# Attention on one core: a slot plan for the other matmuls, five rotating score banks, six value visits per group

## The chip, the core and the metric

The kernel runs on one core of one Trainium2 chip. The metric is the device time of one execution in microseconds (us), taken as the median of several runs. TensorE (PE) multiplies, ScalarE (ACT) evaluates exponentials and casts, VectorE (DVE) and GpSimd (POOL) do elementwise work, and SyncE (SP) issues nearly all transfers. PE writes its results to PSUM, of which a core has eight banks of 128 x 512 float32 values.

## The reference

```python
def _A_ref(x, wq, wk, wv, wo):                     # x: 1 x 2048 x 448, 16 heads of 28
    q = (x @ wq).reshape(B, S, H, Dh).transpose(0, 2, 1, 3)
    k = x @ wk                                     # one key and one value head for all
    v = x @ wv
    scores = jnp.einsum("bhqd,bkd->bhqk", q, k) * (Dh ** -0.5)
    p = softmax(scores, axis=-1)
    o = jnp.einsum("bhqk,bkd->bhqd", p, v)
    return o.transpose(0, 2, 1, 3).reshape(B, S, H * Dh) @ wo

def _B_ref(x, w1, w2, w3, w4):
    h = gelu(layernorm(x) @ w1)
    hs = shift_four_channel_quarters(h, +1, -1, +2, -2) @ w2
    x1 = x + hs
    return x1 + gelu(layernorm(x1) @ w3) @ w4      # 448 -> 1792 -> 448

g = sigmoid((x * gate_w).sum(-1, keepdims=True))
return g * _A_ref(...) + (1 - g) * _B_ref(...)
```

## The kernel before

The first 424 us of the profiled execution compute keys, values, the query projections of the first two groups and all of branch B; `x1` then holds branch B. The change leaves these stages alone. What follows is attention, in the part of the kernel that opens the pools `s3` and `ps3`.

**Groups and key tiles.** Attention is cut into NU = 16 groups `u`: four blocks `b` of 512 queries times four head groups `g` of four heads. In a group the loop runs over NT = 16 key tiles `kt` of 128 keys. For each key tile and each of the four heads `j`, PE computes one score tile `s` (128 keys x 512 queries, line 663), and ACT writes its exponential `p` to SBUF (line 665). Scores and weights are in float32r, products with values in float32.

**Value products.** `pv_group` (lines 618 to 636) multiplies the four `p` tiles of one key tile with `vext` (values and a column of ones) into the four 32-row strips of one PSUM bank `pv` (line 625). The four heads use four column strips of the array. The loop calls it for two key tiles at a time, in every second turn, for the key tiles that lie two and three turns back (LAG = 2, PVB = 2). Such a call is called a visit below: eight visits per group, 16 instruction records each (each product has two records).

**PSUM.** Two banks `mm`, one `misc`, one `mx` (for `pv`), two `m` and two `s`. Score tile n goes to one of five banks by n modulo 5 (`s_tile`; both `mm`, `misc`, both `s`). In the last group it is three banks (n modulo 3), since two `m` and two `s` banks hold the four output accumulators of the last block.

**PE's other work in attention.** PE's order is the order of the program text (`manual_schedule`); the other engines are ordered by the scheduler. Between scores PE has: the 11 matmuls of a query projection (`q_job`, line 503) for the group after the next, whose result is split by ACT and DVE (`q_evac`) and copied by three transfers into `qs`; four parts of the row maximum of the next group (`max_part`, four small matmuls each, line 166, reduced by DVE on line 167), then `max_end` on DVE and one transposing matmul in `max_rows` (line 193); one matmul that spreads the reciprocal sums (`norm_job`, line 543); and for each block four tiles of 12 matmuls of the output projection (`wo_job`, lines 556 to 560), each closed by `gate_out`. All of these use the two `m` banks. `pump()` takes one step of the queue `jobs` after every second score tile. Query jobs are put at the head of the queue; the four output tiles of a block come in one run after the block's last group; the max parts stand outside the queue at key tiles 6 to 9.

**Start of attention.** `wqraw`, block 0 of x (`xq_0`) and `woraw` are loaded to two buffers of tag `raw` and split by DVE and POOL (`split_wq`, `load_x`, lines 485 to 490 and 577 to 593). The later blocks of x are loaded by `load_x` half a group ahead.

**End.** After the last group the bank `pv` is copied by ACT in four parts, transposed, scaled, transposed again and multiplied with the last group's part of `wo` (`tail_a`, `tail_b`, `tail_c`); nine of the twelve matmuls of each output tile of the last block have been done before, in the last group.

Of the kernel before, what the change touches and what calls it, by code (L numbers as in the profile page):

```python
# [15 lines left out]
P = 128  # L16
# [13 lines left out]
LAG = 2  # L30
PVB = 2
# [4 lines left out]
def f32(ap):  # L36
    return ap.bitcast(F32)
# [3 lines left out]
def gated_mix_kernel(  # L41
# [412 lines left out]
    with tc.tile_pool(name="s3", bufs=1, reuse_waits="tile") as s3, \  # L454
# [14 lines left out]
        def s_more(name):  # L469
            return ps3.tile([P, 512], F32, tag="s", bufs=2, name=name)  # L470

# [11 lines left out]
        def load_x(b):  # L483
            raw = s3.tile([P, 4, 512], F32, tag="raw", bufs=2, name=f"xq_{b}")
            nc.sync.dma_start(raw, xT[:, :, 512 * b:512 * b + 512])
            ah = s3.tile([P, 4, 512], F32R, tag="ah", bufs=1, name=f"ahq_{b}")
            al = s3.tile([P, 3, 512], F32R, tag="al", bufs=1, name=f"alq_{b}")
            (nc.gpsimd if b else nc.vector).tensor_copy(ah, raw)
            nc.gpsimd.tensor_tensor(al, raw[:, 0:3, :], f32(ah)[:, 0:3, :], ALU.subtract)
            nc.gpsimd.tensor_tensor(ah[64:128, 3, :], raw[64:128, 3, :], f32(ah)[64:128, 3, :], ALU.subtract)  # L490
            xact[b] = (ah, al)

        def q_job(u):
            b, g = divmod(u, NG)
            ah, al = xact[b]
            cols = slice(g * P, (g + 1) * P)
            ps = misc_tile(f"q_{u}")
            ops = []
            for c in range(3):
                ops += [(wqh[:, c, cols], ah[:, c, :]), (wqh[:, c, cols], al[:, c, :]), (wql[:, c, cols], ah[:, c, :])]  # L500
            ops += [(wqh[:, 3, cols], ah[:, 3, :]), (wql[:, 3, cols], ah[:, 3, :])]
            for n, (w, a) in enumerate(ops):
                nc.tensor.matmul(ps, w, a, start=(n == 0), stop=(n == 10))  # L503
                if n < 10:
                    yield
# [3 lines left out]
            yield  # L509
# [31 lines left out]
        def norm_job(u, o, rb):  # L541
            ps = (mm_tile if u == NU - 2 else misc_tile)(f"rbc_{u}")
            nc.tensor.matmul(ps, sel8, rb, start=True, stop=True)
            on = s3.tile([P, 512], F32, tag="onf", bufs=2, name=f"on_{u}")
            nc.vector.tensor_mul(on, o, ps)  # L545
            onh = s3.tile([P, 512], F32R, tag="onh", bufs=5, name=f"onh_{u}")
            onl = s3.tile([P, 512], F32R, tag="onl", bufs=5, name=f"onl_{u}")
# [3 lines left out]
            yield  # L551

        def wo_group(ps, b, t, g, first, last):
            tok = slice(t * P, (t + 1) * P)
            onh, onl = on_of[b * NG + g]
            nc.tensor.matmul(ps, onh[:, tok], woh[:, g, :], start=first, stop=False)  # L556
            yield
            nc.tensor.matmul(ps, onh[:, tok], wol[:, g, :], start=False, stop=False)  # L558
            yield
            nc.tensor.matmul(ps, onl[:, tok], woh[:, g, :], start=False, stop=last)  # L560

# [5 lines left out]
        def wo_job(b, t):  # L567
            ps = misc_tile(f"wo_{b}_{t}")[:, 0:D]
            for g in range(NG):
                yield from wo_group(ps, b, t, g, g == 0, g == NG - 1)  # L570
                if g < NG - 1:
                    yield
            gate_out(4 * b + t, ps)
            yield

        wqraw = s3.tile([P, 4, 512], F32, tag="raw", bufs=2, name="wqraw")
# [10 lines left out]
        split_wq(2, 4)  # L587
        load_x(0)
        woraw = s3.tile([P, 4, 512], F32, tag="raw", bufs=2, name="woraw")[:, :, 0:D]
        nc.sync.dma_start(woraw, wo.rearrange("(g p) n -> p g n", p=P))  # L590
        split_wq(0, 2)
# [6 lines left out]
        jobs = []  # L598
        current = [None]

        def pump():
            if current[0] is None:
                if jobs:
                    current[0] = jobs.pop(0)()
                    next(current[0])
            else:
                try:
                    next(current[0])
                except StopIteration:
                    current[0] = None  # L610

        def drain():
            while current[0] is not None or jobs:
                pump()
# [3 lines left out]
        def pv_group(k):  # L618
            u, kt = divmod(k, NT)
            if kt == 0:  # L620
                pv_of[u] = max_tile(f"pv_{u}")
            pv = pv_of[u]
            ps = p_of.pop(k)
            for j in range(4):
                nc.tensor.matmul(pv[32 * j:32 * j + 32, :], vext[:, kt, :], ps[j],  # L625
                                 start=(kt == 0), stop=(kt == NT - 1), tile_position=(0, 32 * j))
            if kt == NT - 1 and u < NU - 1:
                o, rb = recip_begin(u, pv_of.pop(u))
                delayed.append((k + 6, lambda: norm_job(u, o, rb)))
                if u == NU - 2:  # L630
                    for t in range(4):
                        delayed.append((k + 10, lambda t=t: wo_last_job(t, NG - 2)))
                elif u % NG == NG - 1:
                    for t in range(4):
                        delayed.append((k + 8, lambda t=t: wo_job(u // NG, t)))

        wo_last = []

        def wo_last_job(t, g):
            if g == 0:  # L640
                wo_last.append((m_tile if t < 2 else s_more)(f"wo_{NB - 1}_{t}")[:, 0:D])
            yield from wo_group(wo_last[t], NB - 1, t, g, g == 0, False)
            yield

        delayed = []
        for k in range(NU * NT + LAG):
            u, kt = divmod(k, NT)
            while delayed and delayed[0][0] <= k:
                jobs.append(delayed.pop(0)[1])
            if k == (NU - 1) * NT:  # L650
                for g in range(NG - 2):
                    for t in range(4):
                        jobs.append(lambda t=t, g=g: wo_last_job(t, g))
            if k < NU * NT:
                if kt == (7 if u == 0 else 2) and u + 2 < NU:
                    jobs.insert(0, lambda u=u: q_job(u + 2))
                if kt == 8 and (u + 3) % NG == 0 and u + 3 < NU:
                    load_x((u + 3) // NG)
                p_of[k] = []
                for j in range(4):  # L660
                    n = 4 * k + j
                    ps = s_tile(n, u == NU - 1)
                    nc.tensor.matmul(ps, kS[0:98, kt * P:(kt + 1) * P], q_of[u][0:98, j, :], start=True, stop=True)  # L663
                    p = s3.tile([P, 512], F32, tag="p", bufs=4 * (LAG + PVB) + 2, name=f"p_{n}")
                    nc.scalar.activation(p, ps, AF.Exp, scale=SCALE)  # L665
                    p_of[k].append(p)
                    if j % 2 == 1 or u == NU - 1:
                        pump()
                if u + 1 < NU:
                    if 6 <= kt < 10:  # L670
                        max_part(u + 1, kt - 6, m_tile)
                    elif kt == 10:
                        max_end(u + 1)
                    elif kt == 11:
                        max_rows(u + 1, m_tile)
# [4 lines left out]
        assert not delayed  # L680
        drain()
# [4 lines left out]
        onh = s3.tile([P, 512], F32R, tag="onh", bufs=5, name=f"onh_{u}")  # L686
        onl = s3.tile([P, 512], F32R, tag="onl", bufs=5, name=f"onl_{u}")
# [20 lines left out]
        def tail_c(t):  # L708
            for _ in wo_group(wo_last[t], NB - 1, t, NG - 1, False, True):
                pass  # L710
            gate_out(4 * (NB - 1) + t, wo_last[t])
# [22 lines left out]
        with tc.If(again > 0):  # L734
            for b in range(NB):
                load_x(b)
                for g in range(NG):
# [7 lines left out]
                    for kt in range(NT):  # L745
                        for j in range(4):
# [3 lines left out]
                            p = s3.tile([P, 512], F32, tag="p", bufs=4 * (LAG + PVB) + 2, name=f"p2_{u}_{kt}_{j}")  # L750
# [59 lines left out]
```

## Time and profile before

| | |
|---|---|
| runs | 1069.8, 1070.5, 1071.85 us; median 1070.5 us |
| profiled execution | 1070.98 us, of which its span (first to last instruction) 1069.1 us |
| mean granted TensorE clock | 0.987 of full speed |
| busy: PE, ACT, DVE, POOL | 1039.7, 673.2, 258.0, 159.8 us |
| attention | the first score starts at 423.94 us |

A line of the timeline reads: start, duration of the merged run of equal instructions, engine, line of the kernel, operation, output <- inputs, shapes, number; in brackets the idle time before it and what ended it. PE's durations overlap, since matmuls are pipelined: the distance of two starts is what an instruction costs PE. In a line of the stages, each engine has its busy time and instruction count, then come the granted clock, the share of busy DMA engines and GB/s.

### The profile page before, as it was taken

To read this page: it belongs to the slowest core of one execution; us is meant where nothing else is said; L and a number is where in the kernel's file an instruction comes from. 1 tells how busy PE (TensorE), PEld (TensorE's weight loads), DVE (VectorE), ACT (ScalarE), POOL (GpSimd) and SP (SyncE) were. 2 spreads that over 40 slices of the span, in tenths; PEclk is the share of its full clock that TensorE was granted. 3 is DMA by queue.
4 is the path that set the end of the run, shared out by engine and by line. 5 is a ranking of instruction groups with operands and counts; after the bars stand their busy time and mean duration, and the time that the engine had idled before them with its cause. 6 is when DMAs were issued, how large, how long until landed. Compare 5 with 4: busy or idle time off the path is not lost.

```text
span 1069.1 us, 13948 instructions
## 1 busy us (share of the span) xinstructions
PE 1039.7 (97%) x5610; PEld 679.6 (64%) x5610; DVE 258.0 (24%) x521; ACT 673.2 (63%) x1318; POOL 159.8 (15%) x182
## 2 busy tenths in 40 slices
PE   6999889999999999999999999999999999999995
PEld 4787778888888888454554555554655555555542
DVE  6744952311411311401110110120110210111102
ACT  5444451222222223788888888889888889888873
POOL 5622430110200201603000002010002100000100
PEclk9999899999999999999999999999999999999998
DMA  9401330000000000423211202220202220211001
GB/s 312 131 1 37 111 111 1 1 1 1 1 1 1 1 1 29 164 32 70 33 17 16 31 20 40 39 31 3 39 10 41 39 31 2 40 24 26 10 2 38
DMA packets 30541, 41.15 MB, mean 38 GB/s; under 512 B 8004, under 2 KB 20100, under 8 KB 30340
## 3 DMA queue, kind: packets, MB, share of 16 engines
q1 hardware_dynamic: 30324, 40.04, 16.3%
q8 instruction: 46, 0.75, 0.3%
q14 instruction: 27, 0.22, 0.1%
q10 hardware_dynamic: 144, 0.13, 0.1%
HBM read 23.28 MB, written 3.67 MB: 25 GB/s over the span
## 4 chain that ended last, share of the span: by engine, by line
PE 91%; DVE 4%; DMA 1%; ACT 1%; POOL 1%; issue 1%; SPq 0%; POOLq 0%; ACTq 0%; DVEq 0%
PE s L663 27%; PE pv L625 22%; PE acc L420 4%; PE acc L419 4%; PE acc L421 4%; PE g L115 4%; PE g L116 4%; PE g L117 4%; PE q L503 3%; PE m L166 2%; PE wo L560 1%; PE wo L558 1%; PE wo L556 1%; PE g L119 1%; PE g L118 1%; PE h L116 1%
## 5 line engine op out<-in xcount | busy, mean ns | idle before, releaser
L665 ACT ACTIVATE p<-s 128x512 f32<-128x512 f32 x1024 | 517.6, 627 | 98.1 <-PE s L663 97.8
L663 PE MATMUL s<-qs,kS 98*128 98x512 f32 x1024 | 343.6, 420 | 1.4 <-ACT p L665 0.7
L663 PEld LDWEIGHTS s<-qs,kS 98*128 98x128 f32 x1024 | 181.6, 189 | 168.2 <-ACT p L665 127.1
L625 PE MATMUL pv<-p,vext 128*32 128x512 f32 x2048 | 247.6, 602 | 0.0
L409 ACT ACTIVATE gh<-g 128x512 fp32r<-128x512 f32 x56 | 33.6, 600 | 174.9 <-PE g L119 174.9
L625 PEld LDWEIGHTS pv<-p,vext 128*32 128x32 f32 x2048 | 53.7, 109 | 107.6 <-issue 100.3
L411 DVE TENSOR_TENSOR gl<-gf,gh 128x512 fp32r<-128x512 f32 x56 | 41.3, 738 | 192.1 <-ACT gf L410 192.0
L419 PE MATMUL acc<-w4h,gh 128*128 128x448 f32 x224 | 82.6, 369 | 0.0
L420 PE MATMUL acc<-w4l,gh 128*128 128x448 f32 x224 | 82.0, 366 | 0.0
L421 PE MATMUL acc<-w4h,gl 128*128 128x448 f32 x224 | 81.7, 365 | 0.0
L167 DVE TENSOR_REDUCE mr<-m 128x4 f32<-128x512 f32 x64 | 44.3, 692 | 146.0 <-PE m L166 145.3
L548 POOL CAST onh<-on 128x512 fp32r<-128x512 f32 x15 | 9.2, 614 | 414.8 <-DVE on L545 228.7
L115 PE MATMUL g<-ah,w3h 128*128 128x512 f32 x168 | 67.1, 399 | 3.1 <-ACT gf L410 2.8
L116 PE MATMUL g<-al,w3h 128*128 128x512 f32 x168 | 66.5, 396 | 0.1
L117 PE MATMUL g<-ah,w3l 128*128 128x512 f32 x168 | 66.3, 394 | 0.0
L521 DVE SCALAR_TENSOR_TENSOR good<-rt,good 128x16 f32<-128x16 f32 x15 | 2.6, 175 | 190.2 <-DMA rt<-o 190.2
L419 PEld LDWEIGHTS acc<-w4h,gh 128*128 128x128 f32 x224 | 42.0, 188 | 4.9
L420 PEld LDWEIGHTS acc<-w4l,gh 128*128 128x128 f32 x224 | 42.1, 188 | 4.8
L421 PEld LDWEIGHTS acc<-w4h,gl 128*128 128x128 f32 x224 | 42.0, 188 | 3.6
L166 PEld LDWEIGHTS m<-kS,qs 96*128 96x128 f32 x256 | 38.4, 191 | 6.3 <-DVE mr L167 1.2
L115 PEld LDWEIGHTS g<-ah,w3h 128*128 128x128 f32 x168 | 31.9, 190 | 9.7 <-ACT gf L410 3.3
L564 DVE SCALAR_TENSOR_TENSOR ot<-wo,gg,x 128x448 f32<-128x448 f32 x16 | 10.9, 682 | 108.0 <-PE wo L560 108.0
(204 smaller groups left out, 1144.4 us busy)
## 6 DMA issues: line engine op xcount, KB each, us to landing
qs<-qh SPq DMA_DIRECT2D x32, 256.0 KB
qs<-ql SPq DMA_DIRECT2D x16, 256.0 KB
xq<-in_xT_dram SPq DMA_DIRECT2D x4, 1024.0 KB
x<-in_x_dram SPq DMA_DIRECT2D x4, 896.0 KB
w3raw<-in_w_dram SPq DMA_DIRECT2D x7, 512.0 KB
out_dram<-ot SPq DMA_DIRECT2D x16, 224.0 KB
w4raw<-in_w_dram SPq DMA_DIRECT2D x7, 448.0 KB
xkv<-in_xT_dram SPq DMA_DIRECT2D x3, 1024.0 KB
```

The lines of the kernel that those rows point to most:

```text
L115: nc.tensor.matmul(ps, wh[:, c, :], ah[:, c, :], start=(c == 0), stop=False)
L116: nc.tensor.matmul(ps, wh[:, c, :], al[:, c, :], start=False, stop=False)
L117: nc.tensor.matmul(ps, wl[:, c, :], ah[:, c, :], start=False, stop=False)
L166: nc.tensor.matmul(ps[:, j, :], q_of[u][0:96, j, t * P:(t + 1) * P], kS[0:96, 0:MK], start=True, stop=True)
L167: nc.vector.reduce_max(mx_of[u][:, :, t], ps, axis=AX.X)
L411: nc.vector.tensor_sub(gl, gf, f32(gh))
L419: nc.tensor.matmul(ps, gh[:, tok], w4h[i][:, k, :], start=(f == 0), stop=False)
L420: nc.tensor.matmul(ps, gh[:, tok], w4l[i][:, k, :], start=False, stop=False)
L421: nc.tensor.matmul(ps, gl[:, tok], w4h[i][:, k, :], start=False, stop=(f == NF - 1))
L625: nc.tensor.matmul(pv[32 * j:32 * j + 32, :], vext[:, kt, :], ps[j], start=(kt == 0), stop=(kt == NT - 1), tile_position=(0, 32 * j))
L663: nc.tensor.matmul(ps, kS[0:98, kt * P:(kt + 1) * P], q_of[u][0:98, j, :], start=True, stop=True)
L665: nc.scalar.activation(p, ps, AF.Exp, scale=SCALE)
```

## The change

The queue `jobs`, `pump` and the delayed jobs are replaced by a fixed plan for each group. A slot follows every second score tile, 32 to a group, and takes one step of the plan. `units(u)` lists pairs (first slot, job), worked off in order, each not before its slot. In most groups: the query job from slot 0, the four max parts from slot 12, the spreading matmul at 16, the row of maxima at 17, one output tile of the block before from slot 18. So the four output tiles of a block are spread over the next four groups, one each. Group 0 has the max parts from slot 4, the row at 12, the query job from 20. All of them use the two `m` banks.

Value products are taken in visits after key tiles 3, 6, 9, 12, 14 and after key tile 0 of the next group (`VISITS`). A visit covers the key tiles up to the one before the current: three key tiles four times, two key tiles twice. The number of `p` buffers stays 18.

Scores rotate over the same five banks as before; the two `s` banks get a name each. In the last group it is four banks instead of three, and only two of the four output tiles of the last block are begun there; the other two are computed whole in the tail, whose steps are put in another order. `raw` has one buffer instead of two, `onh` and `onl` have seven instead of five. Both halves of `wq` are split before block 0 of x is loaded, and block 0 is split by DVE alone but for one small part.

```diff
-LAG = 2
-PVB = 2
+VISITS = (3, 6, 9, 12, 14, 16)
@@
-            return (mm_tile, mm_tile, s_spare, s_more, s_more)[n % (3 if last else 5)](f"s_{n}")
+        def s_more(i):
+            return lambda name: ps3.tile([P, 512], F32, tag=f"s{i}", bufs=1, name=name)
+        s_tiles = (mm_tile, mm_tile, s_spare, s_more(0), s_more(1))
+            return s_tiles[n % (4 if last else 5)](f"s_{n}")
@@ load_x
-            raw = s3.tile([P, 4, 512], F32, tag="raw", bufs=2, name=f"xq_{b}")
+            raw = s3.tile([P, 4, 512], F32, tag="raw", bufs=1, name=f"xq_{b}")
-            (nc.gpsimd if b else nc.vector).tensor_copy(ah, raw)
-            nc.gpsimd.tensor_tensor(al, raw[:, 0:3, :], f32(ah)[:, 0:3, :], ALU.subtract)
+            eng = nc.gpsimd if b else nc.vector
+            eng.tensor_copy(ah, raw)
+            eng.tensor_tensor(al, raw[:, 0:3, :], f32(ah)[:, 0:3, :], ALU.subtract)
@@ start
         split_wq(2, 4)
+        split_wq(0, 2)
         load_x(0)
         nc.sync.dma_start(woraw, wo.rearrange("(g p) n -> p g n", p=P))
-        split_wq(0, 2)
@@ plan
+        def max_units(u):
+            for t in range(4):
+                max_part(u, t, m_tile)
+                if t == 3:
+                    max_end(u)
+                yield
+        def units(u):
+            b, g = divmod(u, NG)
+            wo = [(18, wo_job(b - 1, g))] if b else []
+            norm = [(16, norm_unit(u - 1))] if u else []
+            if u == 0:
+                return [(4, max_units(1)), (12, row_unit(1)), (20, q_job(2))]
+            if u < NU - 2:
+                return [(0, q_job(u + 2)), (12, max_units(u + 1))] + norm + [(17, row_unit(u + 1))] + wo
+            if u < NU - 1:
+                return [(12, max_units(u + 1))] + norm + [(17, row_unit(u + 1))] + wo
+            return ([(0, wo_job(b - 1, g))] + [(12, wo_early(t, g)) for t, g in ((0, 0), (0, 1))] + norm +
+                    [(18, wo_early(t, g)) for t, g in ((1, 0), (1, 1), (0, 2), (1, 2))])
@@ loop
-                    if j % 2 == 1 or u == NU - 1:
-                        pump()
-                if u + 1 < NU:
-                    if 6 <= kt < 10:
-                        max_part(u + 1, kt - 6, m_tile)
+                    if j % 2 == 1:
+                        while True:
+                            if job is None:
+                                if not plan or plan[0][0] > 2 * kt + j // 2:
+                                    break
+                                job = plan.pop(0)[1]
+                            try:
+                                next(job)
+                                break
+                            except StopIteration:
+                                job = None
-            if k >= LAG and k % PVB == PVB - 1:
-                for kk in range(k - LAG - PVB + 1, k - LAG + 1):
-                    if kk >= 0:
-                        pv_group(kk)
+            if kt in VISITS or kt == 0 and u:
+                v = VISITS.index(kt or NT)
+                visit(u if kt else u - 1, VISITS[v - 1] if v else 0, VISITS[v])
@@ tail
+        wo_last.append(m_tile(f"wo_{NB - 1}_2")[:, 0:D])
+        wo_last.append(s_tiles[3](f"wo_{NB - 1}_3")[:, 0:D])
-        for step in range(6):
-            if step < 4:
-                tail_a(step)
-            if 0 < step < 5:
-                tail_b(step - 1)
-            if step > 1:
-                tail_c(step - 2)
+        tail_wo(2, 0)
+        tail_a(0)
+        tail_a(1)
+        tail_wo(2, 1)
+        tail_b(0)
+        tail_b(1)
+        tail_a(2)
+        tail_a(3)
+        tail_wo(2, 2)
+        tail_wo(3, 0)
+        tail_wo(0, 3)
+        tail_wo(1, 3)
+        tail_b(2)
+        tail_b(3)
+        tail_wo(3, 1)
+        tail_wo(3, 2)
+        tail_wo(2, 3)
+        tail_wo(3, 3)
```

More of the change, by code (lines that the diff above doesn't have):

```diff
@@ L543, in norm_job @@
             nc.tensor.matmul(ps, sel8, rb, start=True, stop=True)
+            yield
             on = s3.tile([P, 512], F32, tag="onf", bufs=2, name=f"on_{u}")
             nc.vector.tensor_mul(on, o, ps)
-            onh = s3.tile([P, 512], F32R, tag="onh", bufs=5, name=f"onh_{u}")
-            onl = s3.tile([P, 512], F32R, tag="onl", bufs=5, name=f"onl_{u}")
+            onh = s3.tile([P, 512], F32R, tag="onh", bufs=7, name=f"onh_{u}")
+            onl = s3.tile([P, 512], F32R, tag="onl", bufs=7, name=f"onl_{u}")
             nc.gpsimd.tensor_copy(onh, on)
@@ L560, in wo_group @@
             nc.tensor.matmul(ps, onl[:, tok], woh[:, g, :], start=False, stop=last)
+            yield
         def gate_out(n, ps):
@@ L570, in wo_job @@
                 yield from wo_group(ps, b, t, g, g == 0, g == NG - 1)
-                if g < NG - 1:
-                    yield
             gate_out(4 * b + t, ps)
-            yield
-        wqraw = s3.tile([P, 4, 512], F32, tag="raw", bufs=2, name="wqraw")
+        wqraw = s3.tile([P, 4, 512], F32, tag="raw", bufs=1, name="wqraw")
         nc.sync.dma_start(wqraw, wq)
@@ L587, in gated_mix_kernel @@
         split_wq(2, 4)
+        split_wq(0, 2)
         load_x(0)
-        woraw = s3.tile([P, 4, 512], F32, tag="raw", bufs=2, name="woraw")[:, :, 0:D]
+        woraw = s3.tile([P, 4, 512], F32, tag="raw", bufs=1, name="woraw")[:, :, 0:D]
         nc.sync.dma_start(woraw, wo.rearrange("(g p) n -> p g n", p=P))
-        split_wq(0, 2)
         nc.gpsimd.tensor_copy(woh, woraw)
@@ L596, in gated_mix_kernel @@
             nc.gpsimd.tensor_scalar(x1[:, n, :], x1[:, n, :], gi[:, n:n + 1], None, op0=ALU.mult)
[L598 to L613, printed above, removed]
-                pump()
+        norm_of = {}
@@ new lines, in gated_mix_kernel, with row_unit, norm_unit, wo_early @@
+        wo_last = []
+        def max_units(u):
[3 more added lines that the diff above has]
+                    max_end(u)
+                yield
+        def row_unit(u):
+            max_rows(u, m_tile)
+            yield
+        def norm_unit(u):
+            yield from norm_job(u, *norm_of.pop(u))
+        def wo_early(t, g):
+            if g == 0:
+                wo_last.append((m_tile if t else s_tiles[4])(f"wo_{NB - 1}_{t}")[:, 0:D])
+            yield from wo_group(wo_last[t], NB - 1, t, g, g == 0, False)
@@ new lines, in rest @@
+        def rest():
+            yield
+        def units(u):
[10 more added lines that the diff above has]
+                    [(18, wo_early(t, g)) for t, g in ((1, 0), (1, 1), (0, 2), (1, 2))])
@@ L616, in gated_mix_kernel, with visit @@
         p_of, pv_of = {}, {}
-        def pv_group(k):
-            u, kt = divmod(k, NT)
-            if kt == 0:
+        def visit(u, k0, k1):
+            if k0 == 0:
                 pv_of[u] = max_tile(f"pv_{u}")
             pv = pv_of[u]
[L623 to L646, printed above, removed]
-            u, kt = divmod(k, NT)
[L648 to L653, printed above, removed]
+            for kt in range(k0, k1):
+                ps = p_of.pop((u, kt))
+                for j in range(4):
+                    nc.tensor.matmul(pv[32 * j:32 * j + 32, :], vext[:, kt, :], ps[j],
+                                     start=(kt == 0), stop=(kt == NT - 1), tile_position=(0, 32 * j))
@@ L654, in gated_mix_kernel @@
+            if k1 == NT and u < NU - 1:
+                norm_of[u] = recip_begin(u, pv_of.pop(u))
+        for k in range(NU * NT + 1):
+            u, kt = divmod(k, NT)
             if k < NU * NT:
-                if kt == (7 if u == 0 else 2) and u + 2 < NU:
-                    jobs.insert(0, lambda u=u: q_job(u + 2))
+                if kt == 0:
+                    plan = units(u)
+                    at, job = 0, None
                 if kt == 8 and (u + 3) % NG == 0 and u + 3 < NU:
                     load_x((u + 3) // NG)
-                p_of[k] = []
+                p_of[u, kt] = []
@@ L663, in gated_mix_kernel @@
                     nc.tensor.matmul(ps, kS[0:98, kt * P:(kt + 1) * P], q_of[u][0:98, j, :], start=True, stop=True)
-                    p = s3.tile([P, 512], F32, tag="p", bufs=4 * (LAG + PVB) + 2, name=f"p_{n}")
+                    p = s3.tile([P, 512], F32, tag="p", bufs=18, name=f"p_{n}")
                     nc.scalar.activation(p, ps, AF.Exp, scale=SCALE)
-                    p_of[k].append(p)
-                    if j % 2 == 1 or u == NU - 1:
-                        pump()
-                if u + 1 < NU:
-                    if 6 <= kt < 10:
-                        max_part(u + 1, kt - 6, m_tile)
[L672 to L675, printed above, removed]
-            if k >= LAG and k % PVB == PVB - 1:
-                for kk in range(k - LAG - PVB + 1, k - LAG + 1):
-                    if kk >= 0:
-                        pv_group(kk)
-        assert not delayed
-        drain()
+                    p_of[u, kt].append(p)
+                    if j % 2 == 1:
[9 more added lines that the diff above has]
+                                job = None
+                if kt == NT - 1:
+                    if job is not None:
+                        for _ in job:
+                            pass
+                    for _, job in plan:
+                        for _ in job:
+                            pass
+            if kt in VISITS or kt == 0 and u:
+                v = VISITS.index(kt or NT)
+                visit(u if kt else u - 1, VISITS[v - 1] if v else 0, VISITS[v])
         u = NU - 1
@@ L685, in gated_mix_kernel @@
         o = s3.tile([P, 512], F32, tag="o", bufs=2, name=f"o_{u}")
-        onh = s3.tile([P, 512], F32R, tag="onh", bufs=5, name=f"onh_{u}")
-        onl = s3.tile([P, 512], F32R, tag="onl", bufs=5, name=f"onl_{u}")
+        onh = s3.tile([P, 512], F32R, tag="onh", bufs=7, name=f"onh_{u}")
+        onl = s3.tile([P, 512], F32R, tag="onl", bufs=7, name=f"onl_{u}")
         on_of[u] = (onh, onl)
```

15 lines of the change are left out of this document (5 added, 10 removed).

## The prediction

> **What bounds the kernel now.** I read the page first (busy shares, chain, groups), then the timeline of PE and ACT in attention, because the diff touches nothing else.
>
> ```profile
> PE 1039.7 (97%) x5610; PEld 679.6 (64%) x5610; DVE 258.0 (24%) x521; ACT 673.2 (63%) x1318; POOL 159.8 (15%) x182
> ...
> PE s L663 27%; PE pv L625 22%; PE acc L420 4%; PE acc L419 4%; PE acc L421 4%; PE g L115 4%; PE g L116 4%; PE g L117 4%; PE q L503 3%; PE m L166 2%; PE wo L560 1%; PE wo L558 1%; PE wo L556 1%; PE g L119 1%; PE g L118 1%; PE h L116 1%
> ...
> L665 ACT ACTIVATE p<-s 128x512 f32<-128x512 f32 x1024 | 517.6, 627 | 98.1 <-PE s L663 97.8
> ...
> L167 DVE TENSOR_REDUCE mr<-m 128x4 f32<-128x512 f32 x64 | 44.3, 692 | 146.0 <-PE m L166 145.3
> ```
>
> The chain runs through PE, half of it in scores and value products. But a PE that waits inside a merged run also counts as busy, so the 97% doesn't say whether PE or the score banks set the pace. The distances of starts do. Here are two pairs of key tiles without other work and one with four query matmuls:
>
> ```profile
> 457.27 1.92 PE L625 MATMUL pv<-p,vext 128*32 128x512 f32 x16
> 459.13 2.65 PE L663 MATMUL s<-qs,kS 98*128 98x512 f32 x8
> 461.71 1.92 PE L625 MATMUL pv<-p,vext 128*32 128x512 f32 x16
> ...
> 471.02 1.92 PE L625 MATMUL pv<-p,vext 128*32 128x512 f32 x16
> 472.87 0.73 PE L663 MATMUL s<-qs,kS 98*128 98x512 f32 x2
> 473.44 0.40 PE L503 MATMUL q<-alq,wqh 128*128 128x512 f32 x1
> 473.68 0.63 PE L663 MATMUL s<-qs,kS 98*128 98x512 f32 x2
> 474.15 0.39 PE L503 MATMUL q<-ahq,wql 128*128 128x512 f32 x1
> ...
> 475.56 0.39 PE L503 MATMUL q<-alq,wqh 128*128 128x512 f32 x1
> 475.88 1.92 PE L625 MATMUL pv<-p,vext 128*32 128x512 f32 x16
> ```
>
> Two scores take 474.15 - 473.68 = 0.47, so 0.235 each; a query matmul 473.68 - 473.44 = 0.24, and 0.235 fits the row. A visit of two key tiles holds PE for 1.86 (457.27 to 459.13). The first two scores behind it take 0.57 (472.87 to 473.44) instead of 0.47 (0.10 more), and 0.09 passes between the last query matmul (475.56 + 0.235) and the visit. The full pair is then 1.86 + 0.19 + 12 x 0.235 = 4.87; its rows show 4.86 (471.02 to 475.88). So **a full pair is bound by PE**. The bare pair would be 1.86 + 0.19 + 8 x 0.235 = 3.93, and shows 4.44 (457.27 to 461.71): 0.5 us is a wait. For what, ACT shows:
>
> ```profile
> 424.38 7.95 ACT L665 ACTIVATE p<-s 128x512 f32<-128x512 f32 x16 [5.14 <-PE s L663]
> ...
> 459.66 4.03 ACT L665 ACTIVATE p<-s 128x512 f32<-128x512 f32 x8 [0.42 <-PE s L663]
> ```
>
> Exponentials follow each other at (7.95 - 0.63)/15 = 0.488 and last 0.63; the first begins 0.53 after its score (459.13 to 459.66). With five banks score 8 needs exponential 3 to be over: 0.53 + 2 x 0.488 + 0.63 = 2.14 after the first score. It started some 2.58 - 0.09 - 0.235 = 2.25 after it, so 0.11 goes into the hand-over. **A bare pair is bound by the banks**, and every further score before a visit costs 0.488, not 0.235.
>
> **The change part by part.** *Visits.* Two fewer per group. [...] The last visit before the end, twice as long, gives the price of products; here it is, behind two others of the last group:
>
> ```profile
> 1016.63 1.92 PE L625 MATMUL pv<-p,vext 128*32 128x512 f32 x16
> ...
> 1022.07 1.92 PE L625 MATMUL pv<-p,vext 128*32 128x512 f32 x16
> ```
>
> ```profile
> 1049.91 3.64 PE L625 MATMUL pv<-p,vext 128*32 128x512 f32 x32
> ```
>
> 16 more records take 1.72, so four take 0.43. A pair's products are 1.72 of its 1.86; the switch costs 0.14 + 0.10 + 0.09 = 0.33. Two fewer in 16 groups would be 10.6 us, if PE were the bound. A visit of three key tiles takes 1.86 + 0.86 = 2.72; none is in the trace.
>
> *Stretches of twelve scores.* Four of the six stretches now have 12 scores. Bare, that is 2.58 + 4 x 0.488 = 4.53. Work between the scores hides in the bank waits, except the step behind the last score: that is added. For its price:
>
> ```profile
> 479.25 0.56 PE L166 MATMUL m<-kS,qs 96*128 96x128 f32 x4
> 479.64 0.67 PE L663 MATMUL s<-qs,kS 98*128 98x512 f32 x2
> ```
>
> ```profile
> 648.18 0.37 PE L558 MATMUL wo<-wol,onh 128*128 128x448 f32 x1
> 648.39 0.39 PE L663 MATMUL s<-qs,kS 98*128 98x512 f32 x1
> ```
>
> A max part costs 0.39, an output matmul 0.21. PE's own bill for 12 scores and 6 query matmuls, 12 x 0.235 + 6 x 0.235 + 0.19 = 4.42, lies below the banks' 4.53 + 0.24 = 4.77. So the banks now bind full stretches too.
>
> *Two banks for the rest.* The query tile ends at slot 10 in one `m` bank; the second max part (slot 13) needs it. ACT casts it behind the exponentials it still owes, then DVE subtracts; the third and fourth part wait for DVE's reduction of the first two, and the row at 17 for all four:
>
> ```profile
> 645.67 0.64 ACT L147 CAST qh<-q 128x512 fp32r<-128x512 f32 x1
> ```
>
> ```profile
> 646.34 0.69 DVE L148 TENSOR_TENSOR ql<-q,qh 128x512 fp32r<-128x512 f32 x1 [4.72 <-ACT qh L147]
> ```
>
> Up to five exponentials (2.4) + 0.64 + 0.69 = 3.8, against 6 scores at 0.488 and a max part = 3.3 that PE can do meanwhile: a wait of 0 to 0.5, I take 0.3. For the row: DVE's reduction (0.69, the group of line 167 above) and two short steps, with the spreading product's multiplication in the same queue, some 1.4 to 2.0, against 4 scores and a matmul = 1.2: a wait of 0.2 to 0.8, I take 0.7. Scores, hence ACT, are queued behind both.
>
> A full group (4 to 14) then takes, by stretches (the first visits of groups 3, 4 and 15 stand here and above):
>
> ```profile
> 547.04 1.92 PE L625 MATMUL pv<-p,vext 128*32 128x512 f32 x16
> ```
>
> ```profile
> 585.04 1.92 PE L625 MATMUL pv<-p,vext 128*32 128x512 f32 x16
> ```
>
> Query 4.77; query and max 4.53 + 0.39 + 0.3 = 5.22; max, spreading, row, output by PE's bill 12 x 0.235 + 0.19 + 2 x 0.39 + 0.24 + 0.10 + 2 x 0.21 + 0.7 = 5.25 (the row's matmul at a quarter of a max part, the spreading one as a query matmul); output 4.74; eight scores with four output matmuls 2.91; eight with two query matmuls 2.58 + 0.24 = 2.82. With visits of 4 x 2.72 + 2 x 1.86 = 14.60 this is 40.4. Before, these eleven groups took 1016.63 - 585.04 = 431.6; now 444.4: **+12.8**. Groups 1 to 3 have no output steps: 14.60 + 4.77 + 5.22 + 4.83 + 4.53 + 2.58 + 2.82 = 39.4, where one took 585.04 - 547.04 = 38.0: **+4.2**.
>
> *Group 0.* Its max parts move from key tile 6 to slot 4. The built order has the third one behind score 13, and DVE's reduction of the first behind both halves of `split_wq`, which wait for `wqraw`:
>
> ```profile
> 429.09 0.95 DVE L580 CAST wqh<-wqraw 128x768 fp32r<-128x768 f32 x1 [4.33 <-DMA wqraw<-in_wq_dram]
> ...
> 433.60 1.85 DVE L584 CAST wql<-wqraw 64x256 fp32r<-64x256 f32 x1
> ```
>
> ```profile
> 423.94 6.49 PE L663 MATMUL s<-qs,kS 98*128 98x512 f32 x16
> 430.36 3.51 PE L625 MATMUL pv<-p,vext 128*32 128x512 f32 x16
> ```
>
> ```profile
> 431.00:432.00 1.00, 1.00 (x12) 0.31 (x8) 1.00 (x1) 1.00 (x3) 1.00 (x1) 0.50 0.20 74
> ```
>
> PE is there two scores before the visit of 430.36, at about 429.4; DVE is free at 433.60 + 1.85 = 435.45 and through the reduction at 436.2. PE, and with it ACT, stands still for 6.8 us; then come two max parts, two scores and 0.09, and the first visit starts at 437.5 instead of 430.36. To the next group's first visit it is twice a bare 2.72 + 4.53, then 2.72 + 4.77 with query matmuls, 2.72 + 3.0, 1.86 + 2.82 and 1.86 + 4.77, 39.0 together: 13.6 + 39.0 = 52.6 after 423.94, where before it was 471.02 - 423.94 = 47.1: +5.5. And the granted clock (the last but two of the numbers in the last row): it stood at 0.50 in 431 to 432, after a stretch in which PE streamed 0.235 of every 0.488, and the visit took 3.51 instead of 1.92. The stall is emptier than that; one such half-speed time over two scores, two max parts and half the visit I put at an estimated 2.5 (0.8 + 0.5 + 1.2 more). **+8.0** together; 5.5 if it falls in the stall, 10 if it covers the visit.
>
> [...]
>
> The single `raw` buffer delays `woraw` and the next block of x by one split each; SP's queue behind it (the row of group 1, the copies of query 2) has until the group's end. I cost that at nothing; POOL's splits are cover, and if it is gone, PE waits a few us once.
>
> *Last group and tail.* Three banks gave a pair of 5.44 (1016.63 to 1022.07). Four banks and 12 scores: 2.72 + 4.53 + 0.488 + 0.21 = 7.95 per three key tiles, against 1.5 x 5.44 = 8.16: -0.8 for four. The last visit is shorter by 1.72, and the tail does 18 more output matmuls, 18 x 0.21 = 3.8 if nothing hides them. That is +1.3, or -2.5 if the tail's waits for ACT and DVE hide them all; most stand between scores that no longer come, so I take **+1.0**.
>
> Sum: 8.0 + 4.2 + 12.8 + 1.0 = 26.0. The profiled execution took 1070.98 (span 1069.1), 0.5 above the median of 1070.5; the forecast is 1070.5 + 26.0 = **1096.5 us**.
>
> **The rivals.** *PE is the bound after all, and the visits saved show* (faster). This is so if the twelfth score needs no wait: by PE's bill of a full stretch it would start 4.42 - 0.56 = 3.86 after the first, by the banks 0.53 + 6 x 0.488 + 0.63 + 0.11 = 4.20; exponentials at 0.43 or less decide it. For it: full pairs are PE-bound today, with 0.2 to spare. Against: 0.488 in 16 exponentials in a row. Time: 1070.5 - 10.6 + 8.0 = 1068, by 0.24% faster. [...]
>
> *Only the start is lost.* Groups come out even: spreading the output tiles fills the 0.5 us that each bare pair idles, and that pays for the longer stretches. Time: 1070.5 + 8 = 1078.5. Against: bare or full, a stretch of 12 is held by the banks.
>
> [...]
>
> **How the numbers follow.** Forecast 0.72, PE-bound 0.06, start only 0.10, gate 0.12. The forecast's own bounds: 64 stretches of 12 uncertain by 0.1 each (6), the waits for DVE (0.2 to 1.3 against 1.0 per group, -11 to +4), the start (-2.5 to +2), the tail (-3.5 to +0.3); not all on one side: 1085 to 1108. With the lower gate cases 1085 to 1110, which leaves out the first two rivals and the worst of the third, 0.2 in all. A difference of 0.2% (2 us) is about what a measurement can tell. Faster 0.06, same 0.01, slower 0.93.
>
> **What would show it.** Right: visits of 24 records about 2.78 long and 7.25 to 8.0 apart; groups 1 to 3 at 39.4, full ones at 40.4; a gap on PE before a max part from 429 to 436 ended by DVE line 166. Wrong: full triples at 7.1 or less (PE-bound), no gap at 429, half clock inside groups 1 to 14, or PE waits of over 1 us on `m` banks in each group.

## The result, and the profile after

The changed kernel takes 1117.8 us (median; 1115.5 to 1122.0), where the kernel before takes 1071.2 beside it: a ratio of 1.044, 95% interval 1.040 to 1.048, a loss of 46.7 us. The direction is the one forecast; the forecast loss was 26 us, and the range (to 1110) does not hold the time. The profiled execution took 1122.0 us (span 1120.2); its loss against the profile of before is 51 us, of which 49.1 lie between the first score and PE's end. (It is the longest of the changed kernel's runs, some 4 us above their median.)

The page of the changed kernel (its lines have other numbers: scores stand on line 661, exponentials on 663, value products on 644, max parts and their reduction on 165 and 166, the row's matmul `mt` on 192), its lines for the engines, the exponentials and DVE's reduction of the max parts:

```profile
PE 1069.4 (95%) x5610; PEld 679.3 (61%) x5610; DVE 260.8 (23%) x522; ACT 673.3 (60%) x1318; POOL 158.6 (14%) x181
...
L663 ACT ACTIVATE p<-s 128x512 f32<-128x512 f32 x1024 | 516.8, 641 | 144.6 <-PE s L661 144.2
...
L166 DVE TENSOR_REDUCE mr<-m 128x4 f32<-128x512 f32 x64 | 44.1, 691 | 160.2 <-PE m L165 160.2
```

PE has the same 5610 matmul records, and ACT the same 517 us of exponentials. ACT's idle time before exponentials has grown from 98.1 to 144.6 us: by 46.5, nearly the whole loss. ACT starves because PE hands it scores later; who holds PE has to be read from PE's rows. Its timeline, first the visits that open groups 1, 4 and 15, then those of group 7 (a full group) up to the first of group 8:

```profile
483.07 2.78 PE L644 MATMUL pv<-p,vext 128*32 128x512 f32 x24
...
606.31 2.78 PE L644 MATMUL pv<-p,vext 128*32 128x512 f32 x24
...
731.28 2.78 PE L644 MATMUL pv<-p,vext 128*32 128x512 f32 x24
739.48 2.78 PE L644 MATMUL pv<-p,vext 128*32 128x512 f32 x24
748.27 2.78 PE L644 MATMUL pv<-p,vext 128*32 128x512 f32 x24
755.80 2.78 PE L644 MATMUL pv<-p,vext 128*32 128x512 f32 x24
761.42 1.92 PE L644 MATMUL pv<-p,vext 128*32 128x512 f32 x16
766.16 1.92 PE L644 MATMUL pv<-p,vext 128*32 128x512 f32 x16
772.92 2.78 PE L644 MATMUL pv<-p,vext 128*32 128x512 f32 x24
...
1064.88 2.78 PE L644 MATMUL pv<-p,vext 128*32 128x512 f32 x24
```

The distances of starts in group 7, beside the prediction's pieces (visit and following stretch):

| | query, max | max, spreading, row, output | output | 8 scores, output | 8 scores, query | query | group |
|---|---|---|---|---|---|---|---|
| predicted | 7.94 | 7.97 | 7.46 | 5.63 | 4.68 | 6.63 | 40.3 |
| measured | 8.20 | 8.79 | 7.53 | 5.62 | 4.74 | 6.76 | 41.6 |

Four of six pieces are right within 0.13 us. The second one was forecast 0.82 too short. (The six predicted pieces add up to 40.31; the prediction's sum went on with 40.4, which is 1.0 us more over eleven groups.) By parts of attention, each from the starts above and those of before in the prediction:

| | predicted | measured |
|---|---|---|
| first score to group 1's first visit (57.2, before 47.1) | +8.0 | +10.1 |
| groups 1 to 3 (123.2, before 114.0) | +4.2 | +9.2 |
| groups 4 to 14 (458.6, before 431.6) | +12.8 | +27.0 |
| group 15 and the tail (45.9, before 43.0) | +1.0 | +2.8 |

*The start* went as foretold. PE's rows, then DVE's (a wait in brackets), then the stages with the granted clock:

```profile
425.89 3.55 PE L661 MATMUL s<-qs,kS 98*128 98x512 f32 x10
...
438.11 1.12 PE L165 MATMUL m<-kS,qs 96*128 96x128 f32 x4 [6.72 <-DVE mr L166]
...
440.86 3.83 PE L644 MATMUL pv<-p,vext 128*32 128x512 f32 x24
```

```profile
435.52 1.81 DVE L582 CAST wql<-wqraw 64x256 fp32r<-64x256 f32 x1
437.36 1.29 DVE L166 TENSOR_REDUCE mr<-m 128x4 f32<-128x512 f32 x2
```

```profile
432.00:433.00 1.00, 0.00 (x0) 0.90 0.00 0
...
434.00:435.00 1.00, 0.00 (x0) 0.50 0.00 0
...
443.00:444.00 1.00, 1.00 (x12) 0.98 0.03 12
```

The third max part waits 6.72 us for a reduction that stands behind both splits of the weights. The clock halves in the stall (from about 432.8, 1.4 us after PE ran dry) and stays so through the max parts, two scores and more than half of the first visit, to about 443.

*The row of maxima* is the piece that was too short. PE, DVE and POOL in group 7:

```profile
743.68 0.56 PE L165 MATMUL m<-kS,qs 96*128 96x128 f32 x4
...
744.83 0.63 PE L661 MATMUL s<-qs,kS 98*128 98x512 f32 x2
746.64 0.30 PE L192 MATMUL mt<-identR,mc 128*128 128x128 f32 x1 [1.18 <-DVE mc L185]
```

```profile
744.27 0.69 DVE L166 TENSOR_REDUCE mr<-m 128x4 f32<-128x512 f32 x1 [0.22 <-PE m L165]
745.10 0.69 DVE L546 TENSOR_TENSOR on<-o,rbc 128x512 f32<-128x512 f32 x1
745.71 0.17 DVE L184 TENSOR_SCALAR mc<-mr 128x16 fp32r<-128x16 f32 x1
745.91 0.59 DVE L185 SCALAR_TENSOR_TENSOR mc<-mr,mc 128x16 fp32r<-128x16 f32 x1
```

```profile
745.86 0.61 POOL L549 CAST onh<-on 128x512 fp32r<-128x512 f32 x1 [39.65 <-DVE on L546]
```

The queue on DVE is the one that the prediction named (the spreading product's multiplication ahead of the two short steps), but the last short step takes 0.59 instead of 0.18, beside POOL's cast. The list of waits sums this up (total, times, longest):

```profile
PE mt L192 <- DVE mc L185: 15.1, 14, 1.2
...
PE m L165 <- DVE mr L166: 9.8, 16, 6.7
```

### The profile page after: what moved, and what is told of

The parts are those of the page before. It is cut to its first block, busy times and chain, and to the rows that moved or that the text cites. A ratio compares the mean times of both kernels' runs of the same rounds, so it can differ in the third digit from the quotient of the medians.

```text
span 1120.2 us, 14019 instructions
## 1 busy us (share of the span) xinstructions
PE 1069.4 (95%) x5610; PEld 679.3 (61%) x5610; DVE 260.8 (23%) x522; ACT 673.3 (60%) x1318; POOL 158.6 (14%) x181
## 4 chain that ended last, share of the span: by engine, by line
PE 88%; DVE 7%; DMA 2%; ACT 1%; issue 1%; POOL 1%; SPq 0%; DVEq 0%; POOLq 0%; ACTq 0%
PE s L661 25%; PE pv L644 21%; PE acc L419 4%; PE acc L418 4%; PE acc L420 4%; PE g L114 3%; PE g L115 3%; PE g L116 3%; PE q L505 3%; PE m L165 3%; PE wo L556 1%; PE wo L558 1%; PE wo L560 1%; PE g L118 1%; PE g L117 1%; DVE mr L166 1%
## 5 line engine op out<-in xcount | busy, mean ns | idle before, releaser
L663 ACT ACTIVATE p<-s 128x512 f32<-128x512 f32 x1024 | 516.8, 641 | 144.6 <-PE s L661 144.2
L661 PE MATMUL s<-qs,kS 98*128 98x512 f32 x1024 | 365.3, 431 | 0.1
L644 PEld LDWEIGHTS pv<-p,vext 128*32 128x32 f32 x2048 | 57.8, 111 | 129.7 <-issue 122.6
L165 PE MATMUL m<-kS,qs 96*128 96x128 f32 x256 | 38.3, 273 | 9.8 <-DVE mr L166 9.8
```

Of the source, the lines that this page charges most:

```text
L165: nc.tensor.matmul(ps[:, j, :], q_of[u][0:96, j, t * P:(t + 1) * P], kS[0:96, 0:MK], start=True, stop=True)
```

## The experiments

"Changed" is the changed kernel, 1117.8 us; each time is a median, each ratio against the kernel before, run beside it. Diffs are against the changed kernel where nothing else is said.

**Visits of two key tiles.**

```diff
-VISITS = (3, 6, 9, 12, 14, 16)
+VISITS = (2, 4, 6, 8, 10, 12, 14, 16)
```

> The changed kernel with visits of two key tiles instead of three (eight per group), all else as changed. A (score banks: every score beyond the eighth of a stretch costs 0.488 instead of 0.235): full groups fall from 41.6 to about 40.3 (the old 39.2 and the row's wait of 1.2 that stays), groups 1 to 3 from 41.1 to about 39; with the start and the last group -17 to -24 us, so 1094 to 1101. B (PE is the bound and the loss comes only from the waits for DVE and the start): two more visits per group cost 0.33 each, +10.6, so 1128. C (half clock in stretches that are too empty): shorter stretches trip it less, -3 to -8.

Measured: 1099.3 us, ratio 1.025 (1.022 to 1.028): 18.5 less than changed. Groups 4 to 14 take 446.3 (458.6), and the row's wait is all there in the list of waits:

```profile
PE mt L192 <- DVE mc L185: 15.1, 14, 1.2
```

So the longer stretches cost about 18 us net of the two visits they save; B's 1128 is out by 29. A is not all of it: undisturbed full groups fall from 41.6 to 40.7, not to 40.3, and C has a part, since four half-clock times of the changed kernel's trace, of some 1.6 us each, do not occur in this one (the clock, below).

**The row two slots later.**

```diff
-            wo = [(18, wo_job(b - 1, g))] if b else []
+            wo = [(20, wo_job(b - 1, g))] if b else []
...
-... [(17, row_unit(u + 1))] + wo
+... [(19, row_unit(u + 1))] + wo
```

> The changed kernel with the row's product asked for at key-tile slot 19 instead of 17 and the output steps at 20 instead of 18; triples stay. B (the loss is PE's wait for DVE at the row): the 1.18 us of the 14 rows go, -13 to -17 us, so 1101 to 1105, and the group's fourth stretch with the row falls from 8.8 to about 7.6. A (banks alone): the banks bind those stretches anyway, 0 to -4 us.

Measured: 1099.5 us, ratio 1.025 (1.022 to 1.029): 18.3 less. No wait of `mt` is left, and the stretch (the second in the table above; the expectation calls it the fourth) falls from 8.79 to 7.38, as its visits in group 7 show:

```profile
731.57 2.78 PE L644 MATMUL pv<-p,vext 128*32 128x512 f32 x24
738.95 2.78 PE L644 MATMUL pv<-p,vext 128*32 128x512 f32 x24
```

B is right too: the row costs some 1.35 us in a full group (group 7 falls from 41.64 to 40.29), more than the 1.18 of the wait by itself. The edit also takes two output matmuls out of this stretch, which add 0.05 to a stretch of eight scores. Its trace has two half-clock times where that of changed has five, so a part of the 18.3 is the clock. A alone foresaw at most 4. Neither theory is enough by itself.

**The start's max parts at slot 12.**

```diff
-                return [(4, max_units(1)), (12, row_unit(1)), (20, q_job(2))]
+                return [(12, max_units(1)), (18, row_unit(1)), (20, q_job(2))]
```

> The changed kernel with group 0's max parts asked for at slot 12 and its row at 18 (4 and 12 in the changed one). If the start's loss is the max part that waits for DVE behind the splits of the query weights: the 6.7 us stall goes and with it the half clock of the first two visits, -6 to -10 us (first score to group 1's first visit from 57.2 to 48 to 50). If it is the triples or the clock alone that lengthen the start: 0 to -2 us.

Measured: 1116.0 us, ratio 1.040 (1.036 to 1.045): only 1.9 less, within the spread of the changed kernel. The stall has moved, as DVE and PE show:

```profile
443.92 1.23 DVE L490 CAST ahq<-xq 128x2048 fp32r<-128x2048 f32 x1 [6.68 <-DMA xq<-in_xT_dram]
```

```profile
447.59 1.12 PE L165 MATMUL m<-kS,qs 96*128 96x128 f32 x4 [4.35 <-DVE mr L166]
```

Now the reductions stand behind the split of x, and that waits for its transfer, which the single `raw` buffer holds back until the weights are split. The prediction had costed that buffer at nothing.

**The kernel before with the six visits of the change** (diff against the kernel before, with parts left out; LAG and PVB stay there, since they set the number of `p` buffers):

```diff
+VISITS = (3, 6, 9, 12, 14, 16)
...
-            if k >= LAG and k % PVB == PVB - 1:
...
+            if kt in VISITS or kt == 0 and u:
```

> The kernel before with its eight visits of two key tiles replaced by the six of the change (3, 6, 9, 12, 14, 16); its own order of the other work, its banks and its start stay. A (score banks): +0.9 per full group, +1.5 in the others, about +10 to +25 us, so 1081 to 1096. B (waits for DVE alone): within 3 us of the old time. PE as the bound: two visits fewer in 16 groups, -10.6, so 1060.

Measured: 1104.6 us, ratio 1.029 (1.026 to 1.033): +31, more than A's +10 to +25, and far from PE as the bound (-10.6). Groups 1 to 3 take 40.2 instead of 38.0. Part of the excess is four half-clock times where the kernel before has one, and waits for DVE that it does not have; how the rest divides was not shown:

```profile
PE rbc L544 <- DVE ql L149: 4.7, 8, 0.6
...
PE wo L557 <- DVE ql L149: 3.6, 3, 1.2
```

**Scores on four banks in every group.**

```diff
-            return s_tiles[n % (4 if last else 5)](f"s_{n}")
+            return s_tiles[n % 4](f"s_{n}")
```

> The changed kernel with the scores on four banks in every group (five in groups 0 to 14 of the changed kernel). A (banks): in each of the 60 stretches of twelve scores a score has to wait for an exponential one place later, 60 x 0.488 = +29 us, and up to +15 more from the 30 stretches of eight: 1147 to 1162. PE as the bound: the freed bank stands idle, 0 to +5.

Measured: 1158.7 us, ratio 1.079 (1.077 to 1.082): +40.9, near the upper end of A's +29 to +44. (Ten half-clock times against five in the traces, some 8 us, are in it.) The score's weight load, which stands for the score in the list of waits, waits for exponentials, first in the changed kernel, then with four banks:

```profile
PEld s L661 <- ACT p L663: 68.4, 252, 0.8
```

```profile
PEld s L661 <- ACT p L663: 144.0, 468, 0.8
```

**The start with a buffer of its own.** The start of the third experiment, and:

```diff
-        wqraw = s3.tile([P, 4, 512], F32, tag="raw", bufs=1, name="wqraw")
+        wqraw = s3.tile([P, 4, 512], F32, tag="qs2", bufs=1, name="wqraw")
```

> The changed kernel with group 0's max parts at slot 12, its row at 18, and the raw query weights in the buffer of the third query tile, which is not in use yet, so that the load of x need not wait for their split. If the start's loss (57.2 against 47.1 us from the first score to group 1's first visit) is DVE's queue, first behind the weights, then behind the x that the one raw buffer holds back: both stalls go, -8 to -11 us, 1107 to 1110, and 47 to 49 us. If it is the triples: 0 to -3 us.

Measured: 1108.0 us, ratio 1.035 (1.030 to 1.039): 9.8 less. From the first score (423.47) to group 1's first visit (471.44) it is 48.0, where changed took 57.2. So the start's loss is DVE's queue, in two places, and not the triples.

**All three mended**: pairs, late row, and this start.

> Visits of two key tiles, the row at slot 19 with the output steps at 20, and the start's max parts and raw buffer as in the kernel before this one. If the stretches, the row's wait and the start are all of the loss and do not overlap: 1117.8 - 18.5 - 18.3 - 9 = 1072, at the time before (1062 to 1076; lower where the four banks of the last group help). If something else of the change costs too (the query tile's wait for its bank, the longer tail): 1078 to 1090.

Measured: 1069.7 us, ratio 0.9982 (0.9967 to 0.9997). The three parts, 18.5 + 18.3 + 9.8 = 46.6, come to the whole loss of 46.7. That they do so to 0.1 us is chance: with each loss taken against the kernel before that ran beside it, they are 20.8 + 20.6 + 10.3 = 51.7 and the fall is 48.5. They add up within some 3 us.

**That version with the visits of three again.**

```diff
-VISITS = (2, 4, 6, 8, 10, 12, 14, 16)
+VISITS = (3, 6, 9, 12, 14, 16)
```

> The version with pairs, late row and mended start, with its visits of two key tiles put back to the six visits of the change. It differs from it in the visits alone. A (banks): groups 1 to 3 from 38.6 to 39.8 and full ones from 39.3 to 40.3, the start by 2: +16 to +20 on 1069.7, so 1086 to 1090. If triples are harmless once the row's wait and the start are mended: 1066 to 1072, and by the visits saved 1059.

Measured: 1090.1 us, ratio 1.017 (1.015 to 1.018): +20.4 over the pairs. Nothing but the visits differs, there are no waits for the row and no stall, and the longer visits still lose. Groups without a half-clock time go as A says: 1 to 3 from 38.6 to 39.8, full ones from 39.3 to 40.3. The profiled execution (1094.8, the longest) has three half-clock times, some 5 us of it, where the one with pairs has none.

**The cast on ACT.**

```diff
-            nc.gpsimd.tensor_copy(onh, on)
+            nc.scalar.copy(onh, on)
```

> The changed kernel with the cast of each normalised value tile on ACT instead of POOL. If POOL's cast beside it is why DVE's last step of the row takes 0.58 instead of 0.18: 0.18 in all 16, the row's wait from 1.18 to about 0.78, -4 to -6 us less what ACT's extra 0.6 us per group costs (0 to +5): 1112 to 1119. If it is the operation's own place in the queue: 0.58 stays, and 1118 to 1124.

Measured: 1108.9 us, ratio 1.034 (1.033 to 1.036): 8.9 less. The durations of DVE's last step (min/median/max in ns), first changed, then with the cast on ACT:

```profile
L185 DVE SCALAR_TENSOR_TENSOR mc<-mr,mc x16: 174/584/586, 177.2 to 1035.9; 128x16 fp32r<-128x16 f32 x16
```

```profile
L185 DVE SCALAR_TENSOR_TENSOR mc<-mr,mc x16: 174/175/176, 174.2 to 1026.7; 128x16 fp32r<-128x16 f32 x16
...
  PE mt L192: 10.6, 14
```

PE's wait falls from 15.1 to 10.6 us, and undisturbed full groups from 41.6 to 41.2, as expected of the cast. The other half of the 8.9 lies outside this wait; this trace has two half-clock times in attention where that of changed has five (below), but that the cast is why was not shown.

**The spreading product first** (diff against the version with all three mended):

```diff
-            norm = [(16, norm_unit(u - 1))] if u else []
+            norm = [(12, norm_unit(u - 1))] if u else []
...
-                return [(0, q_job(u + 2)), (12, max_units(u + 1))] + norm + [(19, row_unit(u + 1))] + wo
+                return [(0, q_job(u + 2))] + norm + [(14, max_units(u + 1))] + [(19, row_unit(u + 1))] + wo
```

> The version with pairs, late row and mended start, with the spreading product of the norm at slot 12 and the max parts behind it at 14 (16 and 12 there). If what is left of the waits for DVE is the second max part's wait for the query tile's bank (the stretch with query and max takes 5.54 where PE's bill is about 5.0): that goes, -0.5 in 14 groups, -5 to -8 us, 1062 to 1065. If the spreading product then has to wait for the reciprocals' trip through DMA: 0 to +10. If neither: 1070.

Measured: 1065.2 us, ratio 0.994 (0.992 to 0.995): 4.5 less, just short of the 5 to 8 expected. The wait of the max parts, before the edit and after it:

```profile
PE m L165 <- DVE mr L166: 3.9, 15, 0.3
```

```profile
PE m L165 <- DVE mr L166: 0.5, 2, 0.2
```

With two more slots between the query tile's end and the first max part, DVE has read the query tile before the max parts begin, and they have both `m` banks. This version beats the kernel before by 0.6% and the changed one by 4.7%.

## Why the prediction was half right

*Banks, visits, switches: right.* Bare triples, here one of group 1, take 7.33 where 2.72 + 4.53 = 7.25 was forecast; visits have 24 records and last 2.78:

```profile
499.15 2.78 PE L644 MATMUL pv<-p,vext 128*32 128x512 f32 x24
501.87 4.68 PE L661 MATMUL s<-qs,kS 98*128 98x512 f32 x12
506.48 2.78 PE L644 MATMUL pv<-p,vext 128*32 128x512 f32 x24
```

The first rival (PE as the bound, 1068) falls by three experiments: one bank fewer costs 41 us, and triples cost 31 in the old order and 20 in the mended one. The two visits saved in each group are worth no more than 0.33 us each here (0.14 + 0.10 + 0.09 in the prediction), and the banks take back more. The second rival (groups come out even, 1078.5) falls with them.

*The row's wait: the term that failed most.* "I take 0.7" out of 0.2 to 0.8. The stretch shows 0.82 more than forecast (8.79 against 7.97), so 1.5; taking it away gave 1.35 to 1.4. Over 14 groups the miss is some 10 us. The prediction bounded the waits for DVE by 1.3 us a full group, this one and the next together; they came to 2.1 (1.5 and 0.56), and that alone is 9 us over eleven groups beyond the bound. DVE's bill from the last max part to the row had 2.0 as its longer end; the rows show 2.57 (743.68 + 0.39 to 746.64). In these, 0.41 is the last short step (0.59 for 0.18) and 0.34 are hand-overs (0.20 before the reduction, 0.14 behind the last step); without the two it would be 1.82, inside the bill. Neither end allowed for a short step of 0.59; in the trace of before this step takes at most 0.18 all 16 times.

*The wait of the second max part* was put at 0.3; its stretch is 0.26 longer than forecast, in the 13 groups that have a query projection and max parts: 3.4 us. The prediction also named the wrong release. It has the part wait for the query tile's bank, but in all 13 groups the part starts when DVE has reduced the first part, and before DVE reads the query tile, as PE and DVE show in group 7:

```profile
738.89 0.66 PE L165 MATMUL m<-kS,qs 96*128 96x128 f32 x4 [0.21 <-DVE mr L166]
```

```profile
738.14 0.69 DVE L166 TENSOR_REDUCE mr<-m 128x4 f32<-128x512 f32 x1 [8.30 <-PE m L165]
739.13 0.69 DVE L147 TENSOR_TENSOR ql<-q,qh 128x512 fp32r<-128x512 f32 x1 [0.29 <-ACT qh L146]
```

So the query tile still holds one `m` bank, and the first two max parts share the other.

*The start:* the place and the 6.8 us (6.72 measured) were right, +8.0 became +10.1; a second half-clock time at 456 to 460 makes the third visit 4.48 long. The buffer at "nothing" was wrong in kind. It stayed hidden in the changed kernel behind the stall and decided as soon as the stall was moved.

*The clock: a rival at 0.12 that came true in part.* What the chances and the range of the forecast call "gate", the third rival, is the granted clock falling to half behind bare stretches. It falls to half (0.50) inside the groups too, in the changed kernel three times after group 0. Each time lasts 3.4 us and costs some 1.6. Two follow the row's wait (from 579.6 and from 1037.0); for the first, here are the stages and the visit after them:

```profile
579.00:580.00 1.00, 0.66 (x3) 0.78 0.00 0
580.00:581.00 1.00, 1.00 (x4) 0.50 0.00 0
```

```profile
581.32 3.58 PE L644 MATMUL pv<-p,vext 128*32 128x512 f32 x24
```

Another, in the version with mended start and row but visits of three, follows a bare stretch of twelve scores with no wait for DVE at all. The scores stream 12 x 0.235 = 2.8 of 4.61 us, then the visit lasts 4.48 instead of 2.78:

```profile
530.58 4.68 PE L661 MATMUL s<-qs,kS 98*128 98x512 f32 x12
535.19 4.48 PE L644 MATMUL pv<-p,vext 128*32 128x512 f32 x24
```

Half-clock times between the first score and PE's end, one trace each: before 1, changed 5, with four banks 10, the other kernels with triples 4, 3, 3, 2, 2 and 2; pairs with the start's stall 1, the two mended versions with pairs none. The places differ from trace to trace. The changed kernel's times go with the clock: its runs of 1115.5, 1116.1, 1119.6 and 1122.0 us have mean granted clocks of 0.984, 0.981, 0.979 and 0.977. What starts such a time was not shown. Of the changed kernel's five, one begins 1.4 us after PE ran dry, two 0.2 and 0.3 us behind the row's waits (1.18 and 1.21 long), one (1081.3) 0.7 behind a wait of 0.97 for ACT, and one (456.7) behind a bare stretch of twelve scores. The upper end of the range (1110) took in a part of the case of half clock behind every bare stretch of groups 0 to 3. No run of the changed kernel shows that case: its trace has four half-clock times outside the stall, at some 1.6 us each, and one of them (456.7) is behind such a stretch. The 0.12 was the author's estimate, with one row of before (0.50 in 431 to 432) to go by, and it was too low.

*The last group and tail* gave +2.8; without the half-clock time at 1081 it is 1.2 to 1.3 (this part takes 44.2 to 44.3 us in four of the other kernels with triples), against +1.0.

So of 23 us missing in the profile's sum, some 10 are the row, 3.4 the max part's bank, 4.8 three half-clock times, 2.1 the start, and the rest mostly the 0.06 to 0.13 by which other pieces are short. The signs that the prediction gave as wrong ("half clock inside groups 1 to 14", "PE waits of over 1 us") are both in the trace, the second at the row and not at the `m` banks.

## What to carry to other kernels

Batching the visits of a second kind of work saves switches, but it lengthens the bursts between them, and a burst longer than its buffers ran at the consumer's pace here (0.488 us a score instead of 0.235): price the burst first. Where a plan with fixed slots replaces a queue that fills gaps, every consumer of another engine's result needs slots of distance worked out from that engine's whole queue; here two slots at the row were worth 18 us, half-clock times included. A stall taken away shows the next one behind it, so look for who else is late before a move is called free.

## What the runs showed of the hardware that was not expected

A small DVE operation took 0.59 us instead of 0.17 beside a POOL operation. In the changed kernel `mc` (128x16) takes 0.17 to 0.18 where no cast runs beside it (177.25 and 441.91), and 0.58 to 0.59 all 11 times that POOL's cast has started 0.05 to 0.06 us earlier (745.86 and 745.91 above); in the three cases where DVE starts first, POOL's cast is the longer one, 0.64 for 0.61:

```profile
829.14 0.17 DVE L185 SCALAR_TENSOR_TENSOR mc<-mr,mc 128x16 fp32r<-128x16 f32 x1
```

```profile
829.16 0.64 POOL L549 CAST onh<-on 128x512 fp32r<-128x512 f32 x1 [2.68 <-DVE mc L184]
```

Where POOL starts first, here in group 7, the held step ends at 746.50, the cast at 746.47. With the cast on ACT all 16 steps take 0.18. Where DVE starts first, the cast is held by 0.03 only, though the DVE step had 0.15 to go when the cast started. Why one holds the other was not shown.
